# Smaller score tiles in all steps but the first, and a later load of one weight tile, in a fused attention and low-rank mixer kernel

## The chip, the cores and the metric

The kernel runs on one core of one Trainium2 chip. Its time is the device time in microseconds of one execution. The engines are named as in the profile: PE is TensorE (matmuls), PEld its weight loads, DVE is VectorE, ACT is ScalarE, POOL is GpSimd, and SP is the engine whose queue issues nearly all DMAs here.

## The reference

Two blocks follow each other. The first is causal linear attention with decay, by blocks, for 4 batches, 8 heads, 768 positions and a head width of 64. The second takes its result x (4 x 768 x 512), adds a low-rank mix over positions, and applies a two-layer network with a residual.

```python
for b in range(nb):
    intra = np.einsum('bhic,bhjc->bhij', qb, kb) * Dmask[None]
    intra = np.einsum('bhij,bhjd->bhid', intra, vb)
    inter = np.einsum('bhid,bhde->bhie', qb * lam_pow[None], kv_state)
    out[:, :, sl] = intra + inter
    kv_state = lam_block[None, :, None, None] * kv_state + np.einsum('bhsd,bhse->bhde', kb_dec, vb)
...
h = xt @ U @ V
u = x + h.transpose(0, 2, 1)
ch = np.maximum(u @ w_ch1, 0.0) @ w_ch2
return (u + ch).astype(np.float32)
```

q, k, v and lam are 32-bit floats. U, V, w_ch1 and w_ch2 come as 64-bit floats (two 32-bit words each).

## The kernel before

**Attention, steps 0 to 23.** The kernel works on 128 positions at a time (not the reference's 64): step s is batch s // 6 and position tile s % 6, with all 8 heads. For each step PE does, in small fp32 matmuls:

- `prep`: transposes of the raw q and k tiles (L355), which ACT copies to SBUF (L358);
- `scores`: q times k for every head (L400), into the PSUM tile pss;
- `masked`: DVE multiplies pss by the decay mask into sm (L409), in two halves, x = 0 and 1;
- `inter`: the part from the running state (L441), which needs the state kv and the scaled q (qs, by POOL, L383);
- `intra`: sm times v (L453), added in the same PSUM tile px, which ACT copies to x_nat (L458);
- `state`: the new state (L418 on PE, L426 on DVE).

From step 6 on the mixing of the batch before runs beside it: `low` (L469, once per batch), `mix` (L514 on PE, L517 on DVE: x_nat is changed in place), and `turn`, which transposes (L531), splits into high and low parts (L536, L547 on DVE, L550 on ACT, L551 on POOL), and writes u_d back to DRAM (L534 on SP).

The order on every engine is written out by hand in the list `pieces`. In step s come: prep of s+1, mix, intra of s, state of s, the late ACT work, scores of s+1, inter and masked of s+1, turn. So the scores and the mask of a step are computed one step ahead. SP issues DMAs in this program order too; q and v have three buffers and k has four, so a load is issued when an older tile is free, about three steps before its use.

**The scores' tiles.** A head has 64 columns of q and k, so two heads share the 128 partitions (x selects the half). Up to step 11 one matmul takes 64 rows and 128 columns of weights; from step 12 (`s >= 2 * NT`) it is split in two of 64 x 64, each writing half of the output's partitions. The number of passes per fp32 matmul is two, so the profile counts twice the instructions of the source.

**The weight tiles.** The first network's weights w_ch1 are converted from 64-bit words to three 32-bit parts by `w1_steps`. Its pieces are, for tile 0: four loads of 128 KB (L140), then "one" (L160 and L149 on DVE, and two ACT operations for the exponents, L167 and L168), "two" (L178), "three" (L186), "four" (L191), "five" (L209, then an ACT copy L212), "six" (L217) and "seven" (L224). For tile 1 the second half of "one", `mantissa` (L149), is a piece of its own. The table `side` says in which step each piece runs. `aside(s)` executes those of step s: for s < 12 after `masked`, from step 12 on before `inter` and `masked` (ahead of L409 on DVE). ACT operations of a piece are put on the list `late` and executed in the next step, after its `turned` piece. "One" waits for all four loads.

After step 23 come the first product (L732, L742 on PE, for all of w_ch1, with the conversion of further tiles beside it) and the second product (L865, L867, L869).

Of the kernel before, what the change touches and what calls it, by code (L numbers as in the profile page):

```python
# [14 lines left out]
P = 128  # L15
# [3 lines left out]
def kernel(  # L19
# [32 lines left out]
    NT = S // P  # L52
# [7 lines left out]
    NS = B * NT  # L60
# [136 lines left out]
    def split_steps(tile_of, src, in_parts=False, scale=None, apart=False):  # L197

        st = {}

        def dst():
            if "w" not in st:
                st["w"] = wconv.tile([P, C], FP32, tag="wf", name="wf")
            return st["w"]

        def five():
            st["t"] = t = wconv.tile([P, C], FP32, tag="wt", name="wt")
            st["o"] = o = tile_of()
            nc.vector.tensor_scalar(  # L209
                t.bitcast(U32), st["w"].bitcast(U32), HI, None, ALU.bitwise_and  # L210
            )
            on_scalar(lambda: nc.scalar.copy(o[:, 0, :], t))  # L212

        def six():
            w, low = st["w"], st["o"][:, 1, :]
            st["low"] = low.bitcast(FP32) if scale is None else w
            nc.vector.tensor_tensor(  # L217
                out=low if scale is None else w, in0=w, in1=st["t"], op=ALU.subtract
            )
            if scale is not None:  # L220
                on_scalar(lambda: nc.scalar.mul(low, w, scale))

        def seven():
            nc.vector.scalar_tensor_tensor(  # L224
                st["o"][:, 2, :], st["t"], -E, st["low"], ALU.mult, ALU.add
            )

        return weight_steps(dst, src, C, in_parts=in_parts, apart=apart) + [five, six, seven]
# [3 lines left out]
    def w1_steps(ft, in_parts=False, apart=False):  # L232
        def tile_of():
            w1v[ft] = w1_pool.tile([P, 3, C], F32R, tag="w1", name="w1")
            return w1v[ft]

        cols = moe_w_ch1[:, ft * P : (ft + 1) * P].rearrange("(c p) f -> p c f", p=P)
        return split_steps(tile_of, cols, in_parts, apart=apart)
# [13 lines left out]
    def two_banks(name, tag):  # L252
        return psf.tile([P, 2, N], FP32, tag=tag, name=name)
# [83 lines left out]
    half = [slice(0, D), slice(D, P)]  # L337
# [56 lines left out]
    def scores(s):  # L394
        qt, kt = st[s]["qt"], st[s]["kt"]
        st[s]["pss"] = pss = two_banks("pss", "pss").rearrange("p x (a i) -> p x a i", a=HP)
        for a in range(HP):
            for x in range(2):
                for rows in half if s >= 2 * NT else [slice(0, P)]:
                    nc.tensor.matmul(  # L400
                        out=pss[rows, x, a, :], lhsT=kt[half[x], a, rows],
                        rhs=qt[half[x], a, :], start=True, stop=True,
                    )
# [182 lines left out]
    def load_next(name, engine=nc.sync):  # L586
# [3 lines left out]

    run = {
        "prep": prep, "fade": fade, "scores": scores, "masked": masked, "inter": inter,
        "intra": intra, "state": state,
        "low": low, "low_rows": low_rows, "next_of_low": next_of_low, "mix": mix, "turn": turn,
        "scale": scale, "turned": lambda s: turned.pop(s)(),
    }
    def v_steps():

        st = {}

        def dst():
            if "v" not in st:
                st["v"] = wconv.tile([P, C], FP32, tag="wf", name="vf")[0 : 2 * R, 0:SH]
            return st["v"]

        def parts(gs):
            for half in range(2):
                rows, cols = slice(half * R, (half + 1) * R), slice(half * SH, (half + 1) * SH)
                for g in gs:
                    yield v_hl[g * R : (g + 1) * R, cols], rows  # L610

        def five():
            st["t"] = t = wconv.tile([P, C], FP32, tag="wt", name="vt")[0 : 2 * R, 0:SH]
            nc.vector.tensor_scalar(
                t.bitcast(U32), st["v"].bitcast(U32), HI, None, ALU.bitwise_and
            )
            on_scalar(lambda: high(0))

        def high(g, copy=nc.scalar.copy):
            for out, rows in parts((g,)):  # L620
                copy(out, st["t"][rows])

        def low(g, engine):
            for out, rows in parts((g,)):
                engine.tensor_tensor(
                    out=out, in0=st["v"][rows], in1=st["t"][rows], op=ALU.subtract
                )

        halves = [moe_V[:, half * SH : (half + 1) * SH] for half in range(2)]
        return weight_steps(dst, halves, SH, 2 * R, in_parts=True) + [  # L630
            five, lambda: low(1, nc.vector), lambda: high(2, nc.vector.tensor_copy),
            lambda: low(3, nc.gpsimd),
        ]
# [6 lines left out]
    for steps, at in (  # L640
        (u_side, (-1, 1, 1, 2, 2)),
        (v_steps(), (0, 0, 3, 3, 4, 4, 4, 5, 4, 5)),
        (w1_steps(0, True), (3, 4, 5, 6, 8, 9, 10, 11, 13, 14, 15)),
        (w1_steps(1, True, True), (8, 9, 10, 11, 16, 17, 19, 20, 21, 22, 23, NS)),
    ):
        assert len(steps) == len(at)
        for step, n in zip(steps, at):
            side.setdefault(n, []).append(step)
# [320 lines left out]
```

## Time and profile before

| | |
|---|---|
| Median of 3 runs | 673.42 us (672.98 to 673.69) |
| The profiled execution: time, span | 673.08 us, 671.3 us |
| Busy: PE, PEld, DVE | 665.1, 544.9, 497.1 us |
| Busy: ACT, POOL | 277.3, 112.1 us |
| Granted PE clock | 1.00 |
| PE, scores L400: 64 x 128 tiles, 64 x 64 tiles | 192 of 297 ns, 384 of 275 ns |
| DVE, mask L409 | 48, 30.9 us |
| SP, words L140: 128 KB | 8 issues, 4.0 us to landing (median) |
| Attention's last L453 begins | 119.2 us |

The engines run side by side, so the times are not added. An engine's idle time is put down in brackets to what released it, in the form "[0.24 <-DVE ut L536]". In the timeline the first column is the start in microseconds from the span's beginning and the second the time it took; "x16" is the number of instructions merged into one line. "SPq" is SP's queue of DMA issues, and its time is that of the issue, not of the transfer.

### The profile page before, as it was taken

How to read it: one execution, taken by the hardware profiler on the slowest of the kernel's cores; microseconds unless marked ns; L12 is line 12 of the kernel's file. 1: busy time of each engine (PE TensorE's matmuls, PEld its weight loads, DVE VectorE, ACT ScalarE, POOL GpSimd, SP SyncE). 2: the span in 40 equal slices, each digit the busy share in tenths (PEclk: the TensorE clock that was granted, in tenths of full speed). 3: DMA queues.
4: the chain of work that ended last, by engine and by line, in shares of the span. 5: the costliest groups of instructions: out<-in, count | busy, mean ns of one | idle time of the engine just before them, and what ended most of it. 6: DMA issues, size and time to landing. Idle time of an engine off the chain costs nothing.

```text
span 671.3 us, 13171 instructions
## 1 busy us (share of the span) xinstructions
PE 665.1 (99%) x5124; PEld 544.9 (81%) x5124; DVE 497.1 (74%) x873; ACT 277.3 (41%) x517; POOL 112.1 (17%) x92
## 2 busy tenths in 40 slices
PE   9999999999999999999999999999999999999997
PEld 7888989788888888888888888888888888888886
DVE  4689989877999777777797255786586775865864
ACT  4675767454555444444454121232222322322320
POOL 4465667340000000000000000030030300300300
PEclk9999999999999999999999999999999999999999
DMA  8999993254776555555577899854363363543431
GB/s 198 218 247 239 225 231 113 90 208 157 244 273 234 205 203 205 204 204 205 203 282 254 318 319 388 287 178 151 94 217 97 112 203 94 168 146 95 159 92 63
DMA packets 131775, 131.27 MB, mean 196 GB/s; under 512 B 81346, under 2 KB 89794, under 8 KB 131714
## 3 DMA queue, kind: packets, MB, share of 16 engines
q1 hardware_dynamic: 130512, 130.05, 61.2%
q8 instruction: 40, 0.66, 0.4%
q10 hardware_dynamic: 1202, 0.39, 0.2%
q14 instruction: 21, 0.17, 0.1%
HBM read 80.09 MB, written 50.33 MB: 194 GB/s over the span
## 4 chain that ended last, share of the span: by engine, by line
PE 97%; DVE 1%; DMA 1%; ACT 0%; issue 0%; ACTq 0%; DVEq 0%
PE pz L732 27%; PE pz L867 13%; PE pd L742 13%; PE pz L865 13%; PE pd L869 13%; PE px L453 4%; PE pss L400 4%; PE put L531 2%; PE pq L355 2%; PE px L441 2%; PE pk L355 1%; PE pkv L418 1%; PE pp L469 1%; PE pu L514 1%; DMA kraw<-in_k_dram 1%
## 5 line engine op out<-in xcount | busy, mean ns | idle before, releaser
L732 PE MATMUL pz<-u_hl,w 128*128 128x512 f32 x768 | 190.4, 397 | 0.0
L732 PEld LDWEIGHTS pz<-u_hl,w 128*128 128x128 f32 x768 | 144.0, 188 | 35.4 <-issue 0.4
L867 PE MATMUL pz<-w_hl,m 128*128 128x512 f32 x384 | 151.1, 396 | 0.0
L865 PE MATMUL pz<-w_hl,m 128*128 128x512 f32 x384 | 150.9, 396 | 0.0
L869 PE MATMUL pd<-w_d,m 128*128 128x512 f32 x384 | 149.5, 396 | 0.0
L848 ACT ACTIVATE m<-mt 128x512 fp32r<-128x512 f32 x96 | 60.5, 632 | 197.0 <-PE pd L869 148.9
L849 DVE SCALAR_TENSOR_TENSOR m<-rm,m 128x512 fp32r<-128x512 f32 x96 | 71.4, 746 | 53.7 <-ACT m L848 53.6
L894 POOL TENSOR_TENSOR o<-o,u 128x512 f32<-128x512 f32 x20 | 29.8, 1522 | 447.4 <-DVE o L890 447.4
L747 DVE SCALAR_TENSOR_TENSOR r<-pd,r 128x512 f32<-128x512 f32 x96 | 61.8, 686 | 53.2 <-ACT r L738 38.8
L742 PE MATMUL pd<-u_d,w 128*128 128x512 f32 x384 | 98.6, 397 | 0.0
L738 ACT ACTIVATE r<-pz 128x512 f32<-128x512 f32 x96 | 52.1, 596 | 92.7 <-PE pz L732 92.6
L867 PEld LDWEIGHTS pz<-w_hl,m 128*128 128x128 f32 x384 | 72.3, 188 | 17.7
L865 PEld LDWEIGHTS pz<-w_hl,m 128*128 128x128 f32 x384 | 72.3, 188 | 17.6
L869 PEld LDWEIGHTS pd<-w_d,m 128*128 128x128 f32 x384 | 72.3, 188 | 17.6
L742 PEld LDWEIGHTS pd<-u_d,w 128*128 128x128 f32 x384 | 72.1, 188 | 17.3
L850 DVE SCALAR_TENSOR_TENSOR m<-m 128x512 fp32r<-128x512 f32 x96 | 69.0, 721 | 0.9
L847 DVE TENSOR_SCALAR mt<-rm 128x512 uint32<-128x512 uint32 x96 | 46.1, 481 | 27.3 <-DMA rm<-r_d 26.9
L409 DVE TENSOR_TENSOR sm<-pss,mask 128x512 f32<-128x512 f32 x48 | 30.9, 685 | 7.9 <-PE pss L400 7.7
L212 ACT CAST w<-wt 128x512 fp32r<-128x512 f32 x32 | 19.9, 620 | 30.6 <-DVE wt L209 23.4
L383 POOL TENSOR_TENSOR qs<-qt,powq 128x512 f32<-128x512 f32 x20 | 26.0, 1298 | 22.0 <-ACT qt L358 19.0
L453 PEld LDWEIGHTS px<-vraw,sm 128*64 128x64 f32 x768 | 24.5, 138 | 5.2 <-issue 2.0
L400 PE MATMUL pss<-qt,kt 64*64 64x128 f32 (+1 forms) x576 | 28.1, 283 | 0.0
(88 smaller groups left out, 682.3 us busy)
## 6 DMA issues: line engine op xcount, KB each, us to landing
r_d<-r SPq DMA_DIRECT2D x96, 256.0 KB, 2.5
rm<-r_d SPq DMA_DIRECT2D x96, 256.0 KB, 2.7
words<-in_moe_w_ch_dram SPq DMA_DIRECT2D x30, 512.0 KB, 4.4
w_d<-w SPq DMA_DIRECT2D x16, 768.0 KB, 3.3
w_hl<-w_d SPq DMA_DIRECT2D x16, 512.0 KB, 6.6
vraw<-in_v_dram SPq DMA_DIRECT2D x24, 256.0 KB, 4.8
u_d<-x_nat SPq DMA_DIRECT2D x24, 256.0 KB, 3.6
u<-u_d SPq DMA_DIRECT2D x24, 256.0 KB, 3.8
```

Of the source, the lines that this page charges most:

```text
L400: nc.tensor.matmul(out=pss[rows, x, a, :], lhsT=kt[half[x], a, rows], rhs=qt[half[x], a, :], start=True, stop=True,)
L453: nc.tensor.matmul(out=px[half[t], x, a, :], lhsT=sm[:, x, a, half[t]], rhs=vr[:, 2 * a + x, :], start=(first and a == 0), stop=(a == HP - 1),
L732: nc.tensor.matmul(out=acc[g][0], lhsT=w[:, n, ct, :], rhs=uhl[g][:, n, ct, :], start=(ct == 0 and n == 0), stop=(ct == CT - 1 and n == 1),)
L738: nc.scalar.mul(rs[g], acc[g][0], 4096.0 + 1.0)
L742: nc.tensor.matmul(out=acc[g][1], lhsT=w[:, 2, ct, :], rhs=ud[g][:, ct, :], start=(ct == 0), stop=(ct == CT - 1),)
L747: nc.vector.scalar_tensor_tensor(rs[g], acc[g][1], 4096.0, rs[g], ALU.mult, ALU.add)
L848: nc.scalar.activation(out=m[:, 0], in_=t, func=AF.Relu)
L849: nc.vector.scalar_tensor_tensor(m[:, 1], r, 0.0, hi, ALU.max, ALU.subtract)
L850: nc.vector.scalar_tensor_tensor(m[:, 2], hi, E, low, ALU.mult, ALU.subtract)
L865: nc.tensor.matmul(out=pz, lhsT=m[:, 0, cols], rhs=hl[:, 0], start=first, stop=False)
L867: nc.tensor.matmul(out=pz, lhsT=m[:, 1, cols], rhs=hl[:, 1], start=False, stop=end)
L869: nc.tensor.matmul(out=pd, lhsT=m[:, 2, cols], rhs=dd, start=first, stop=end)
```

## The change

It has three parts. The scores are computed on 64 x 64 tiles in every step but step 0 (before: from step 12 on). The four loads of the words of weight tile 1 run in steps 11 to 14 (before: 8 to 11). "Seven" of tile 0 goes from step 15 to 16, and "one" of tile 1 from step 16 to 15. All else, the order of the other pieces included, stays.

```diff
-                for rows in half if s >= 2 * NT else [slice(0, P)]:
+                for rows in half if s > 0 else [slice(0, P)]:
                     nc.tensor.matmul(
                         out=pss[rows, x, a, :], lhsT=kt[half[x], a, rows],
                         rhs=qt[half[x], a, :], start=True, stop=True,
...
-        (w1_steps(0, True), (3, 4, 5, 6, 8, 9, 10, 11, 13, 14, 15)),
-        (w1_steps(1, True, True), (8, 9, 10, 11, 16, 17, 19, 20, 21, 22, 23, NS)),
+        (w1_steps(0, True), (3, 4, 5, 6, 8, 9, 10, 11, 13, 14, 16)),
+        (w1_steps(1, True, True), (11, 12, 13, 14, 15, 17, 19, 20, 21, 22, 23, NS)),
```

## The prediction

> **What bounds the kernel now.** I read the busy line and the chain of the page first, then the groups by form, the timeline of two neighbouring steps, and the waits.
>
> ```profile
> PE 665.1 (99%) x5124; PEld 544.9 (81%) x5124; DVE 497.1 (74%) x873; ACT 277.3 (41%) x517; POOL 112.1 (17%) x92
> ...
> PE 97%; DVE 1%; DMA 1%; ACT 0%; issue 0%; ACTq 0%; DVEq 0%
> ```
>
> TensorE (PE) is never free: it is busy 99% of the span and is 97% of the chain. After 119 us its waits add up to under 2 us. So what the attention part (0 to 119 us, steps 0 to 23) saves on PE should arrive at the end, unless another engine makes PE wait. Below, "step s" is the time from the first L453 matmul of step s to that of s+1; it holds the scores of s+1.
>
> The groups by form show what an L400 instruction costs in both tilings, and the timeline shows step 9 (old form) and step 13 (new form):
>
> ```profile
> L400 PE MATMUL pss<-qt,kt 64*128 64x128 f32 x192 | 14.9, 297 | 0.0
> ...
> L400 PE MATMUL pss<-qt,kt 64*64 64x128 f32 x384 | 13.2, 275 | 0.0
> ...
> 53.08 1.16 PE L400 MATMUL pss<-qt,kt 64*128 64x128 f32 x16
> ...
> 54.80 0.66 PE L531 MATMUL put<-ident,x_nat 128*128 128x128 f32 x4
> ...
> 73.34 1.10 PE L400 MATMUL pss<-qt,kt 64*64 64x128 f32 x32
> ...
> 74.84 0.66 PE L531 MATMUL put<-ident,x_nat 128*128 128x128 f32 x4
> ```
>
> Reader: a line's first number is its start. From the first score to the first matmul after L441 it is 54.80 - 53.08 = 1.72 us in the old form and 74.84 - 73.34 = 1.50 in the new, twice the instructions notwithstanding: **0.21 us a step**. Whole steps agree: 4.95 us (51.53 to 56.49) against 4.73 (71.80 to 76.53), with the same other work on PE.
>
> VectorE (DVE) is the engine that can eat it. In steps 5 and 6 it runs without a gap from 30.87 to 42.37:
>
> ```profile
> 38.34 0.42 DVE L489 TENSOR_SCALAR p_h<-p_f 32x512 uint32<-32x512 uint32 x1
> ...
> 39.17 1.19 DVE L495 TENSOR_TENSOR vp<-p_f,p_h 32x512 fp32r<-32x512 f32 x1
> ...
> 40.40 1.29 DVE L409 TENSOR_TENSOR sm<-pss,mask 128x512 f32<-128x512 f32 x2
> ...
> 41.57 1.06 PEld L453 LDWEIGHTS px<-vraw,sm 128*64 128x64 f32 x32 [0.25 <-issue]
> ```
>
> L409 ends at 41.69; the L453 that reads it began at 41.57 and took 1.06 us instead of its usual 1.01. There PE already runs at DVE's pace.
>
> The third place is where the words of the second weight tile are read:
>
> ```profile
> 65.28 0.79 SPq L140 DMA_DIRECT2D words<-in_moe_w_ch_dram  x1
> ...
> 78.19 2.16 SPq L279 DMA_DIRECT2D vraw<-in_v_dram  x1
> ...
> 80.46 0.79 SPq L534 DMA_DIRECT2D u_d<-x_nat  x1
> ...
> 83.00 0.43 DVE L426 TENSOR_TENSOR kv<-pkv,faded 128x256 f32<-128x256 f32 x1
> ...
> 83.34 0.68 DVE L224 SCALAR_TENSOR_TENSOR w<-wt,w 128x512 fp32r<-128x512 f32 x1
> ...
> 87.74 0.42 DVE L426 TENSOR_TENSOR kv<-pkv,faded 128x256 f32<-128x256 f32 x1 [0.54 <-PE pkv L418]
> ...
> 88.08 0.66 DVE L160 TENSOR_SCALAR sc<-words 128x512 uint32<-128x512 uint32 x1
> ...
> 94.94 1.25 PEld L469 LDWEIGHTS pp<-x_nat,u_w 128*32 128x32 f32 x48 [0.64 <-ACT qt L358]
> ```
>
> The last words were issued at 65.28, far ahead of L160 at 88.08. The bracket on L469 is a wait of PE on ScalarE (ACT) in step 17.
>
> **What the Trainium skill says.** "TensorE: Matmul & The Clock Gate", section The mechanism: tiles at different positions of the array compute at once, and a weight load overlaps matmuls in flight only when its row group differs. The trace agrees that it pays: 32 matmuls of 275 ns need less time than 16 of 297. "Runtime: NRT & Kernel Launch", Instruction fetch mechanics: instructions come in blocks of 16 KiB, 256 each, fetched by DMA while the current ones run, "mostly hidden". The trace has 40 instruction packets of 0.66 MB together, 16 KiB each, and one PE stall that nothing else explains, 0.53 us at 22.0, 2 us after a late packet at 20.35. "SBUF — State Buffer", Who interferes with whom: a DVE operation with two SBUF inputs is held up by a GpSimd (POOL) operation. The trace agrees: L186 takes 0.68 us alone and 1.36 beside L372 at 60.45.
>
> **The change part by part.**
>
> *Scores 1 to 11.* They add 11 x 8 = 88 matmuls, 176 records in the page's count (two per matmul), and as many weight loads. Gross gain 11 x 0.21 = 2.3 us. What of it stays:
> - Scores 1 to 5 (steps 0 to 4): 5 x 0.21 = 1.05. Here the inputs are close behind: raw v of step 4 was issued at 21.87 and took 5.3 us, landing at 27.17, and is needed at 28.11 - 4 x 0.21 = 27.27. q of step 3 lands at 16.84 and is needed at 17.66 - 0.42 = 17.24. Both just hold. Instruction blocks come faster: a step of 105 matmuls and 105 loads becomes 242 instructions in 4.08 us, so 256 last about 4.3 us instead of 5.2. The existing stall may move, vanish or double: from -0.5 (then v of step 4 binds instead) to +0.8. I charge 0.1 and count 0.95.
> - Scores 6 and 7 (steps 5, 6): nothing. DVE's gapless chain from 30.87 to 41.69 keeps its length, so the L453 of step 7 waits what PE saved, up to 0.42.
> - Scores 8 to 11 (steps 7 to 10): 4 x 0.21 = 0.84. DVE has room: 3.4 to 4.3 us busy of 4.74, and each L409 still waits 0.6 for its scores. Step 11's wait of 0.41 on x_nat keeps its distance to scores 11.
>
> *Operation "seven" (L224) from step 15 to 16, "one" (L160) from 16 to 15.* On DVE 0.68 against 0.43 to 0.66, a swap. The two exponents on ACT (L167, L168, 0.72 each) go with "one" and run a step later in its late list: now in step 17, 92.95 to 94.42, delaying the copy of q (L358) that pp L469 waits for; afterwards in step 16, where ACT idles 1.92 us before L358. The copy then starts when its transposes end, near 94.0 instead of 94.33: **gain 0.3**.
>
> *Words from steps 8 to 11 to 11 to 14.* Four issues on SP of 128 KB. Steps 8 to 10 lose one each, which nobody waited for. In steps 12 to 14, SP issues q, k, v and u_d for 0.39 + 0.65 + 2.15 + 0.88 = 4.1 us of 4.73; another 0.8 to 1.1 fills it, so u_d, and next q, slip by under 1 us. q and k are three steps ahead of their use, and the u_d write two steps ahead of the reuse of its buffer, so these are hidden. But the **fourth words** are issued in step 14 behind v, at about 80.4 to 80.9 on the old clock, and landed after 3.0 to 4.8 us in the eight old cases: 83.4 to 85.7. L160 now stands where L224 began, 83.4. It waits 0 to 2.3 us; I take 1.2 (landing 84.6). Behind it on DVE stand sm (L409), ut, u_hl, x_nat and kv. L160 ends at 84.6 + 0.66, sm's second half at 86.57; L453 wants it 0.13 after 86.00: PE stalls 0.45. kv then ends near 88.9, where L441 starts at 88.82 after that stall: 0.15 more. **Loss 0.6**. Up to a wait of some 0.55 the slack of DVE (0.54 before kv at 87.74, 0.7 before L453) covers it; a wait of 2.3 costs 1.7.
>
> Sum: -0.95 - 0.84 - 0.30 + 0.60 = **-1.5 us**. The profiled execution took 673.08, 1.8 us of it outside the span of 671.3; it becomes 671.6. It lies 0.34 below the median of the three runs, 673.42, so the median becomes **671.9**.
>
> **The rivals.** "Within 0.2%" means 672.07 to 674.77; 0.2%, 1.35 us, is about what a measurement of this kernel can tell from no change.
> 1. *The words are hidden*: they land by 84.0. Then the 0.6 is not paid: -2.1, and with luck at scores 6 and 7, -2.4. About 671.2. For it: the lighter queue in steps 8 to 10, and a landing of 3.4 us at 65.28. Against: v's issue of 2.16 shows the rings full there. Chance 0.27.
> 2. *The early part is fed too slowly*: v of step 4 or instruction blocks absorb half of the first 0.95, and the words wait 2 us (1.4). Sum -0.5 - 0.84 - 0.30 + 1.4 = -0.2, with part of it -0.8: 672.9. Tiles that bring nothing under full DMA rings, so that the change does not do what it says, end here too. Chance 0.20.
> 3. *Slower: instruction fetch.* Counting 256 records back from the stall puts the request of the late block near 17.7, so it was some 4.8 us until use (an estimate). Blocks now last 4.3 us in steps 1 to 4 and about 4.8 in 5 to 11. If the mean delay under DMA traffic is above 5.2, each of some ten blocks stalls 0.4 to 0.5: +4.5 against -1.5: 676.4. The sign turns from about four stalls on; it is slower by 0.2% from seven. Against: steps 12 to 18, already 252 instructions per 4.73 us at a DMA share of about 1.0, show no such stall. Chance 0.08.
>
> **How the numbers follow.** Likeliest, with 0.45: 671.9, its own range 671.3 to 672.5, two thirds of it below 672.07. Faster: 0.27 + 0.30 = 0.57; same: 0.15 + 0.20 = 0.35; slower 0.08. The range 670.9 to 673.3 takes in rivals 1 and 2 and leaves out the slower case and the ends.
>
> **What would show it.** Right: steps 7 to 10 last 4.74 us; the L453 of step 7 shows a wait of 0.3 to 0.4 on sm L409; L160 stands behind kv in step 15 with idle time put down to the words' DMA; L469 of step 17 waits 0.3 instead of 0.64. Wrong: PE waits put down to issue at several places before 60 us (rival 3), L453 waiting for vraw (rival 2), no idle before L160 (rival 1), or steps of 64x64 scores before step 12 that stay at 4.9 us.

## The result, and the profile after

The changed kernel takes 676.71 us (median of 22 runs, 674.39 to 680.7) against 673.74 us (22 runs, 672.59 to 678.36) for the kernel before on the same chip: ratio 1.004, interval 1.0026 to 1.0054. The forecast was 671.9, with a range of 670.9 to 673.3; the outcome is the one that the prediction gave 0.08. The profiled execution of the changed kernel took 678.94 us with a span of 677.2.

First the page of the kernel after, its busy line and its chain, against those shown of before:

```profile
PE 665.6 (98%) x5300; PEld 544.9 (80%) x5300; DVE 497.8 (74%) x873; ACT 277.8 (41%) x517; POOL 112.8 (17%) x92
...
PE 94%; DMA 2%; ACT 1%; issue 1%; DVE 1%; SPq 0%; DVEq 0%; ACTq 0%
```

The 176 records more are there (5124 to 5300), yet PE is not busier: 665.1 to 665.6. The span grew by 5.9 us, nearly all of it waiting. From the first L732 to the end both take the same, 550.9 and 551.0 us, so everything lies in attention: from its first to its last L453 it went from 109.19 to 115.62 us.

The groups by form and the waits of the kernel after (name, waited-for: total us, times, longest) say that the tiles are as fast as forecast, and where PE stands instead:

```profile
L400 PE MATMUL pss<-qt,kt 64*64 64x128 f32 x736 | 25.9, 276 | 0.8 <-issue 0.8
```

```profile
PEld px L441 <- issue: 5.8, 6, 1.7
```

276 ns each, as before (275). But L441 waited six times for nothing that the profile shows. The timeline of PEld in the kernel after gives the places (start, time, what, and in brackets the idle time before it):

```profile
21.18 0.52 PEld L400 LDWEIGHTS pss<-qt,kt 64*64 64x64 f32 x18 [1.03 <-issue]
...
40.36 0.54 PEld L441 LDWEIGHTS px<-kv,qs 64*64 64x64 f32 x26 [1.15 <-issue]
...
45.51 0.43 PEld L441 LDWEIGHTS px<-kv,qs 64*64 64x64 f32 x20 [0.56 <-issue]
...
56.63 0.59 PEld L441 LDWEIGHTS px<-kv,qs 64*64 64x64 f32 x32 [1.73 <-issue]
...
76.93 0.47 PEld L441 LDWEIGHTS px<-kv,qs 64*64 64x64 f32 x20
78.84 0.31 PEld L441 LDWEIGHTS px<-kv,qs 64*64 64x64 f32 x12 [1.44 <-issue]
...
84.22 0.31 PEld L441 LDWEIGHTS px<-kv,qs 64*64 64x64 f32 x11 [0.47 <-issue]
...
91.49 0.90 PEld L453 LDWEIGHTS px<-vraw,sm 128*64 128x64 f32 x28 [0.27 <-DVE sm L409]
...
100.09 1.25 PEld L469 LDWEIGHTS pp<-x_nat,u_w 128*32 128x32 f32 x48 [0.37 <-ACT qt L358]
...
104.98 0.20 PEld L441 LDWEIGHTS px<-kv,qs 64*64 64x64 f32 x5 [0.48 <-issue]
```

The reader is to see that most stalls fall in the **middle** of a group of equal instructions (20 of 32 L441, a pause of 1.44 us, the other 12). Data are not what is missing there: the other 12 read the same two tiles as the first 20. The exception is 56.63, ahead of a whole group: that one is kv, late by way of ACT and u_d, told below.

Counting PE's records (matmuls and weight loads) from the start, the pauses within a group stand at 688, 1444, 1700, 1952, 3469, 3720 and 4732: 688 plus a multiple of 252.8 to within three records. The trace also holds PE's semaphore instructions (about three per step), which the views leave out. Counted with them, the seven pauses lie 3, 1, 1, 6, 1 and 4 times 256 apart, exactly: **every 256 instructions, the block of the instruction fetch**. So do the pauses put down to "issue" in the middle of a group in all other kernels of this document. One more view ties a pause to its packet, the DMA queues of the kernel after from 75.7 to 77.5 us (packets, MB, share of 16 engines):

```profile
q8 instruction: 1, 0.02, 5.2%
```

5.2% of 16 engines for 1.8 us is 1.5 us for this packet on its one engine; narrower windows put its start at 75.80, so it ended at 77.3, and PE went on at 78.84. The same in every such pause of the kernel after: PE goes on 1.2 to 1.6 us after the end of a packet. In the kernel before one packet was late in this way (timeline of PEld, before):

```profile
22.54 0.19 PEld L441 LDWEIGHTS px<-kv,qs 64*64 64x64 f32 x3 [0.67 <-issue]
```

After, the pauses of this kind sum to 5.4 us (the seventh, not shown above, is 0.27 in an L469 at 35.30).

### The profile page after: what moved, and what is told of

It is laid out like the page before. It is cut to its first block, busy times and chain, and to the rows that moved or that the text cites. A ratio compares the mean times of both kernels' runs of the same rounds, so it can differ in the third digit from the quotient of the medians.

```text
span 677.2 us, 13523 instructions
## 1 busy us (share of the span) xinstructions
PE 665.6 (98%) x5300; PEld 544.9 (80%) x5300; DVE 497.8 (74%) x873; ACT 277.8 (41%) x517; POOL 112.8 (17%) x92
## 4 chain that ended last, share of the span: by engine, by line
PE 94%; DMA 2%; ACT 1%; issue 1%; DVE 1%; SPq 0%; DVEq 0%; ACTq 0%
PE pz L732 27%; PE pz L867 13%; PE pd L742 13%; PE pz L865 13%; PE pd L869 13%; PE px L453 3%; PE pss L400 3%; PE put L531 2%; PE pq L355 1%; PE px L441 1%; PE pkv L418 1%; PE pk L355 1%; PE pp L469 1%; DMA qraw<-in_q_dram 1%; DMA u_d<-x_nat 1%
## 5 line engine op out<-in xcount | busy, mean ns | idle before, releaser
L732 PE MATMUL pz<-u_hl,w 128*128 128x512 f32 x768 | 190.5, 397 | 0.0
L732 PEld LDWEIGHTS pz<-u_hl,w 128*128 128x128 f32 x768 | 144.0, 188 | 35.5 <-issue 0.4
L453 PEld LDWEIGHTS px<-vraw,sm 128*64 128x64 f32 x768 | 24.6, 138 | 5.7 <-DVE sm L409 2.3
```

The lines of the kernel that those rows point to most:

```text
L732: nc.tensor.matmul(out=acc[g][0], lhsT=w[:, n, ct, :], rhs=uhl[g][:, n, ct, :], start=(ct == 0 and n == 0), stop=(ct == CT - 1 and n == 1),)
```

## The experiments

"First to last" is the time from the first to the last L453 of the profiled execution. "Delay" is the time from PE's first instruction of a new block (by the count with the semaphore instructions) to the start of the next instruction packet. The "rings" are the queues in which the pieces of the transfers wait for the DMA engines. Ratios are to the kernel before in the same session, as recorded, with their 95% interval; they are not exactly the quotients of the medians. Steps, pauses and delays are those of one profiled execution of each kernel.

**Each part alone.** `e1_scores_only` keeps the score tiles only (`half if s > 0`, the table `side` as before); `e2_moves_only` keeps the words and the exchange only (`s >= 2 * NT`).

> Only the first part of the change: scores 1 to 11 on 64 x 64 tiles; words and the two operations as before. Fetch theory (PE waits at the ends of 256-instruction blocks because full DMA rings delay the next block, and the added instructions use blocks up faster): nearly the whole loss, +1.5 to +4 us against before, with waits put down to issue about 253 records apart. Words theory (the later loads of the words and what they displace in the DMA queue make the loss): -1.5 to -2.3 us.

> Only the second and third part: words in steps 11 to 14, L224 and L160 exchanged; scores as before. Fetch theory: within 0.6 us of before (0.3 gained at L469 of step 17, up to 0.6 lost at L160). Words theory: +2 to +4 us.

e1: 675.27 against 672.32 us, ratio 1.0039 (1.0026 to 1.0052). e2: 673.17, ratio 1.0011 (0.9998 to 1.0025). So the scores' tiles, the part meant to save most, make the whole loss. Steps without a pause do save: steps 1 to 3 of e1 last 4.07 to 4.08 instead of 4.29. But e1 pauses at records 1952, 3217, 4226 and 4733, for 0.99, 0.26, 0.72 and 1.07 us. e2 has no pause of the kind, and shows the wait for the words on the way that was forecast, but nearly twice as long. Its timelines of DVE and of PEld:

```profile
83.97 0.43 DVE L160 TENSOR_SCALAR sc<-words 128x512 uint32<-128x512 uint32 x1 [2.12 <-DMA words<-in_moe_w_ch_dram]
```

```profile
85.05 0.20 PEld L453 LDWEIGHTS px<-vraw,sm 128*64 128x64 f32 x4 [0.87 <-DVE sm L409]
...
85.64 0.90 PEld L453 LDWEIGHTS px<-vraw,sm 128*64 128x64 f32 x28 [0.40 <-DVE sm L409]
```

L160 waits 2.12 us, both halves of sm come late, and steps 15 and 16 take 5.37 and 5.25 us instead of 4.73 and 4.74: 1.15 lost.

**Larger pieces.** `e3_after_2k_rows` (the changed kernel) and `e4_before_2k_rows` (the kernel before) read q, k and v as whole rows of 2 KB instead of 8 pieces of 256 B (the tiles then hold other values; no instruction of PE changes):

```diff
-                in_=source[b, h : h + n, c * P : (c + 1) * P, :].rearrange("h p d -> p h d"),
+                in_=source[b].rearrange("h s d -> (h s d)")[
+                    (c * H + h) * P * D : (c * H + h + n) * P * D
+                ].rearrange("(p h d) -> p h d", h=n, d=D),
```

> The changed kernel, but the loads of q, k and v read 2 KB contiguous rows instead of 256-byte pieces: same bytes, an eighth of the descriptors, other data in the tiles, so the attention computes on other values; no instruction of PE, DVE, ACT or POOL is changed. Fetch theory: the DMA share falls well below 1, the waits at block ends vanish, and the kernel is 1.5 to 2.3 us faster than the kernel before with the same loads. Words theory: the same, as the words land early too; then the wait of L160 goes. A theory by which the 64 x 64 form itself is slow in the early steps: still slower than the kernel before with 2 KB rows by 2 us or more.

> The kernel before with the same 2 KB rows for q, k and v (other data in the tiles, as in the run beside it). Fetch theory: its one late block (0.53 us) goes and little else changes, -0.3 to -1.5 us. If the DMA rings bound the early steps in other ways, more.

e3: 672.92, ratio 1.0003 (0.9992 to 1.0014); e4: 671.78, ratio 0.9986 (0.9978 to 0.9994). Lighter traffic takes most of the loss away, but the changed kernel stays the slower one, and still pauses four times (0.85, 0.44, 0.75, 0.42). Traffic has a share; packets do not simply stand behind many small pieces, for the mean delay in steps 12 to 22 is 1.79 us with 2 KB rows and 1.78 without.

**How many instructions, and where a block ends.** From step 12 on a step has 250 records and mostly three semaphore instructions, almost one block, so the end of a block stays near one place of the step. In the kernel before this is in L453, 0.8 us into the step; 352 instructions more (one block and 96) bring it into L441, at 2.8 us. `e5_eight_steps` adds exactly one block (64x64 tiles also in steps 2 to 5 and 8 to 11). `e6_place_only` adds 96 instructions that do nothing, ahead of attention (25 small matmuls in place of one larger idle one), and changes no tile. `e7_eight_steps_swap` is e5 with L224 in step 16 and L160 in step 15, words in 8 to 11. `e8_all_steps_place` has small tiles in all steps but the first and 160 idle instructions ahead of them (42 small matmuls for two larger ones), which bring the end of the block back into L453.

```diff
+                for rows in half if s >= 2 * NT or s in (2, 3, 4, 5, 8, 9, 10, 11) else [slice(0, P)]:   # e5, e7
...
+    for i in range(25):                                            # e6; e8: 42
+        nc.tensor.matmul(out=fill[0:32, 0:2], lhsT=blank[:, 0:32], rhs=blank[:, 0:2], start=True, stop=True)
```

> The kernel before with the new tiles in eight of the eleven steps only, scores 2 to 5 and 8 to 11: 8 x 32 = 256 more instructions on PE, exactly one block, so that from step 12 on the block ends fall at the same place in a step as in the kernel before. Place theory (a block waits when its end falls among the L441, since the request for the next block then queues behind the loads of v): steps 12 to 22 last 4.73 to 4.74 us as before, and the kernel is 0.5 to 1.7 us faster than before. Rate theory (more instructions per microsecond are the cause): stalls in steps 1 to 11 as in the run with all eleven, and a loss of 1 to 2.5 us.

> The kernel before with scores, words and conversion untouched, and 96 more PE instructions ahead of the first transposes: 25 dummy matmuls of 32 x 2 for one dummy matmul of 128 x 128 taken away (about 0.9 us against some 1 us). In the change the 352 added instructions move the block ends of the later steps by 352 - 256 = 96, and here they move by the same. Place theory: waits at block ends in steps 8 to 19 though no rate is changed, 1 to 3 us slower than before. Rate theory: within 0.6 us of before, no new waits.

> As the eight steps, and L224 in step 16 and L160 in step 15 as in the change, but the words stay in steps 8 to 11. L160 should find its words there; the wait of L469 in step 17 falls from 0.64 to 0.37. Both theories: 0.3 us faster than the eight steps alone. If the exchange itself costs DVE time, slower than the eight steps.

> All eleven new score steps (words and conversion as before), and 160 more PE instructions ahead of the first transposes (42 dummy matmuls of 32 x 2 for two of 128 x 128): 352 + 160 = 512, two whole blocks, so the later block ends lie as in the kernel before. Place theory: steps 12 to 22 without waits at block ends, 1 to 2 us faster than the run with the scores alone. Rate theory: as slow as the scores alone (+2.6 us).

e5: 672.59 against 672.64, ratio 1.0003 (0.999 to 1.0016). e6: 676.31, ratio 1.0055 (1.0041 to 1.007). e7: 672.35, ratio 1.0002 (0.9989 to 1.0015). e8: 674.56, ratio 1.0031 (1.002 to 1.0043). Of the two forecasts for e5 neither came true: it is as fast as the kernel before. Its steps 12 to 22 are as they were (but for step 17, 5.99), yet in the early steps a pause of 0.83 at 30.12 and the longer steps 11 and 17 take back most of what its tiles save. The fillers cost more than I had thought: the first L453 of e6 starts at 12.45 and of e8 at 13.83, where the others have 8.5 to 11.0. So these two medians are no measure of the place; the steps are. e6 does the very same work as the kernel before, and gets two pauses that it does not have (timelines of PEld, e6):

```profile
71.85 0.32 PEld L441 LDWEIGHTS px<-kv,qs 64*64 64x64 f32 x14 [0.47 <-issue]
```

```profile
102.00 0.20 PEld L441 LDWEIGHTS px<-kv,qs 64*64 64x64 f32 x6 [0.52 <-issue]
```

Steps 12 and 18 take 5.39 and 5.44 instead of 4.74. Its first to last is 109.58, only 0.4 above the kernel before, as it lacks that one's early pause: so the two pauses, 1.35 us by the steps, are the place's doing, and most of the 3.7 us between the medians is not (its first L453 starts 2.45 us later). e8 has all the small tiles of the changed kernel and no pause after 25.61; its first to last is 107.17, the shortest of all kernels with every load, 4.2 below e1. Its lead in the prologue helps its first steps, so not all of the 4.2 is the place's doing; but its steps 13 to 22 are clean, and those of e1 are not.

`e9_nine_steps` and `e10_ten_steps` move the place without fillers; `e11_swap_only` is the kernel before with the exchange alone.

```diff
+                for rows in half if s >= 2 * NT or s in (1, 2, 3, 4, 5, 8, 9, 10, 11) else [slice(0, P)]:   # e9; e10: 6 too
...
-        (w1_steps(0, True), (3, 4, 5, 6, 8, 9, 10, 11, 13, 14, 15)),
-        (w1_steps(1, True, True), (8, 9, 10, 11, 16, 17, 19, 20, 21, 22, 23, NS)),
+        (w1_steps(0, True), (3, 4, 5, 6, 8, 9, 10, 11, 13, 14, 16)),      # e7, e9, e10, e11
+        (w1_steps(1, True, True), (8, 9, 10, 11, 15, 17, 19, 20, 21, 22, 23, NS)),
```

> The kernel before, with 64x64 score tiles also in steps 1 to 5 and 8 to 11 (288 instructions of TensorE more, 256 + 32), L224 in step 16 and L160 in step 15, the words' loads where they were (steps 8 to 11). From step 12 on a block of 256 instructions then ends some 32 instructions earlier in each step than before, near position 14, at the start of L453. If the place of the block's end decides (theory): steps 12 to 22 stay at 4.73 to 4.74, as that place is still ahead of v's load; the steps 0 to 10 gain 0.21 each less what one or two early stalls take, 671.3 to 672.2 against 672.6 before. If the rate alone decides (rival): stalls as in the changed kernel in steps 7 to 13, 2 to 3 us slower.

> As the nine steps, with step 6 too (320 instructions more, 256 + 64): a block then ends some 64 instructions earlier in each step, near position 234, behind L441, among the transposes for the next step. Theory: the next block is asked for about when v's 1024 pieces are in the rings, so stalls of 0.4 to 0.7 come in two or more of the steps 7 to 20, 1 to 3 us slower than the nine steps although the code differs by 32 instructions. Rival (rate): within 0.3 us of the nine steps.

> The kernel before with the exchange alone: L224 in step 16, L160 in step 15, words' loads in steps 8 to 11, scores as before (no instruction of TensorE more). Step 17 loses 0.26 to 0.3, L160 waits for no DMA, everything else as before: 0.2 to 0.4 us faster than before. Its distance to the run that moved the words too (0.5 us over before) is then the price of the later words, 0.7 to 1.0. Rival: L160 ahead of L409 in step 15 delays sm, so that step 15 takes 0.2 to 0.4 more and nothing is gained.

e9: 673.16 against 673.45, ratio 0.9999 (0.9983 to 1.0016). e10: 675.01, ratio 1.002 (1.0008 to 1.0031). e11: 673.12, ratio 0.9992 (0.9979 to 1.0004). Thirty-two instructions in step 6 part e9 from e10 by 1.9 us. e9 has no pause of the fetch in attention, e10 four (0.48, 0.82, 0.82 and 0.49), two of them in steps 7 and 13, as the theory of the place wanted; beyond step 13 it has none. The gain that I expected of e9 did not come: steps 3, 9 and 10 lose it again (4.82, 5.43, 5.69) to waits for other engines. The one of step 9 is put down to "issue", but it stands ahead of a whole group, not at the end of a block, and ACT had waited for u_d just before (timelines of ACT and PEld, e9):

```profile
51.23 0.58 ACT L458 COPY x_nat<-px 128x512 f32<-128x512 f32 x1 [1.85 <-DMA u_d<-x_nat]
```

```profile
51.88 0.59 PEld L441 LDWEIGHTS px<-kv,qs 64*64 64x64 f32 x32 [0.66 <-issue]
```

It is the same chain as at 56.63 in the kernel after. In the profiled execution e10 also waited 1.61 us for a q tile in step 0, so its first to last (111.59) overstates the pauses. e11 gains in step 17 what was forecast (5.38 instead of 5.65), and its L160 waits for no DMA. By medians e2 lies 0.2% above e11 (1.0011, 0.9992; the intervals overlap a little); 0.2% would be about 1.2 us for the later words, as against 1.15 in e2's steps.

**Does the place matter because of v's load?** My next theory was that a block ending in L441 asks for the next one just when the 1024 pieces of v's load, issued behind the state's matmuls, fill the rings. Moving only that issue to the end of the step tests it: `e12_after_v_late` in the changed kernel, `e13_all_v_late` the same with the words' loads in steps 8 to 11, `e14_swap_v_late` in e11.

```diff
-        load_next("v")
+        if s < 5:
+            load_next("v")
...
+        step += [("load_v", s)] * (s >= 5)      # last in the step, behind turn
```

> The changed kernel with v's load issued at the end of a step, behind u_d, instead of behind the state's matmuls, from step 5 on. If the instruction packet queues behind v's pieces (theory): the block that ends in L441, some 3.3 us into the step, is now followed by a request ahead of v's pieces, the packets of steps 12 to 22 start within 4 us of the step instead of 4.5 to 6.1, and the stalls of 0.47 to 1.44 in steps 9 to 18 go: 2 to 4 us faster than the changed kernel, 673 to 674.5. Rival (it is the rate, or L441 itself): the same stalls, 676 to 677.

> As the last one, with the words' loads back in steps 8 to 11 (all steps on 64x64 tiles, the exchange, v's load late). Theory: no L160 wait, no stalls from step 8 on; 0.7 to 1.0 below the last one, 672 to 673.5. Rival: stalls as before, 675 to 676.

> The kernel before with the exchange and v's load issued at the end of a step from step 5 on; TensorE's instructions as in the kernel before, so a block ends in L453 at the start of a step, now just behind the issue of v's load. Theory: the packets of steps 12 to 22 start later in the step, at 3 to 5 us instead of 1.0 to 2.4, and stalls of 0.4 to 1 appear in two or more steps: 0.5 to 3 us slower than the exchange alone. Rival: no change, within 0.3 us of it.

e12: 676.1 against 674.47, ratio 1.004 (1.0025 to 1.0055); e13: 676.43, ratio 1.0039 (1.0019 to 1.006); e14: 673.26, ratio 0.9984 (0.9971 to 0.9997). **The theory falls**, in both directions. e12 keeps the loss and has the longest pause of all (timeline of PEld, e12; L442 is L441 here):

```profile
106.06 0.20 PEld L442 LDWEIGHTS px<-kv,qs 64*64 64x64 f32 x4 [2.09 <-issue]
```

and e14, whose requests should have come to stand behind v, has no pause of the fetch and the best ratio of the kernels that leave the loads as they are in kind and number, though not one that its interval tells from e11's. The mean delay does not move as the theory wants: 2.04 in e12 (changed kernel: 1.78), 1.10 in e14 (e11: 0.85).

**Queueing at all?** `e15_after_no_v` is the changed kernel without v's loads from step 9 on, `e16_after_no_qkv` without those of q, k and v, `e17_before_no_qkv` the kernel before without them (older tiles are used again, so they compute on other values).

```diff
     def load(name, s, engine):
+        if s >= 9:                       # e15: and name == "v"
+            raw[s, name] = kept[name, s % (4 if name == "k" else 3)]
+            return
```

> The changed kernel without v's loads from step 9 on (the tiles of steps 6 to 8 are used again, so x is another one); TensorE's instructions as in the changed kernel. If the packets wait among data in the rings (theory, without v's special part): the mean delay from block end to packet in steps 12 to 22 falls from 1.9 to about 1.2 us, no stall put down to issue from step 12 on: 2 to 3 us faster than the changed kernel. Rival (the delay comes from the engine's side): still 1.6 to 2.2 us.

> As the last one, with no load of q, k or v from step 9 on: only u_d and the words use the rings. Theory: mean delay under 0.8 us, packets of 0.9 us, no stall from step 9 on, steps 12 to 22 at 4.73. Rival: mean delay still 1.6 to 2.2 us; a stall would then still come now and then.

> The kernel before without loads of q, k and v from step 9 on: the other place of the block end, with empty rings. Theory: mean delay 0.3 to 0.8 us, as in the changed kernel without these loads (the place no longer matters), where the kernel before has 1.0. Rival: 1.0, unchanged, or under half of what the changed kernel without the loads shows.

e15: 672.45 against 673.46, ratio 0.9982 (0.9968 to 0.9997); e16: 671.18, ratio 0.997 (0.9958 to 0.9981); e17: 670.91, ratio 0.9962 (0.9947 to 0.9977). The DMA queues of the kernel after from 74 to 98 us (steps 13 to 16) and of e16 from 60 to 100 us (steps 11 to 19), in packets, MB and share of 16 engines, show how empty the rings became:

```profile
q1 hardware_dynamic: 15549, 5.34, 87.5%
```

```profile
q1 hardware_dynamic: 1584, 2.49, 17.9%
```

With it the mean delay falls from 1.78 (kernel after) to 1.05 (e15) and 0.30 (e16), and the pauses from step 12 on from 2.4 us to 0.26 and none. So the delay depends on the data in the rings: e15 and e16 as expected, far below the rival's 1.6. By medians e16 and e17 differ by 0.3 us (671.18, 670.91): without the loads the loss is gone, but the forecast gain does not show either. These kernels have fewer semaphore instructions (e16 and e17 mostly one in a step), so their blocks hold more records, and the ends of blocks move on in the step. The delays in steps 12 to 22 together (10 or 11 blocks each):

| Kernel | Block ends, us into the step (median) | Mean delay (largest) | Pauses from step 12 on |
|---|---|---|---|
| before | 0.8 | 1.05 (2.40) | none |
| e8, all small tiles, place moved back | 0.8 | 0.82 (1.91) | none |
| e9, nine steps | 0.3 | 1.11 (1.69) | none |
| e14, exchange, v late | 0.8 | 1.10 (2.14) | none |
| e17, before without q, k, v | 1.1 | 0.36 (0.73) | none |
| after | 2.8 | 1.78 (3.38) | 1.44, 0.47, 0.48 |
| e1, scores only | 2.8 | 1.76 (3.19) | 0.26, 0.72, 1.07 |
| e3, after, 2 KB rows | 2.8 | 1.79 (2.39) | 0.75, 0.42 |
| e6, place only | 2.8 | 1.69 (2.13) | 0.47, 0.52 |
| e10, ten steps | 3.9 | 1.29 (3.08) | 0.49 |
| e12, after, v late | 2.8 | 2.04 (4.14) | 0.58, 2.09 |
| e13, as e12, words in 8 to 11 | 2.8 | 1.66 (3.02) | 0.53, 0.26 |
| e15, after without v | 2.9 | 1.05 (1.68) | 0.26 |
| e16, after without q, k, v | 3.4 | 0.30 (1.15) | none |

A block must be there one block after it was asked for. Delay, packet (0.9 to 2.4 us) and the 1.2 to 1.6 us behind it must fit into the block that runs meanwhile. In the pause at 78.84: 3.38 + 1.49 + 1.4 = 6.27 us, where the block that ran meanwhile lasted from 72.43 to 77.40, 4.97 us: 1.30 too late; the pause is 1.44. In e12 at 106.06: 4.14 + 1.59 + 1.4 - 4.92 = 2.21; it is 2.09. The rule sorts all 396 blocks of attention in the 19 traces of this case. Where a packet ended over 1.5 us before the running block ran out, PE never stood at the block's end for more than the 0.24 us that it spends ahead of L453 anyway (335 blocks); where it ended under 1.1 us before, PE always paused, by over 0.2 us (33 blocks); in between 7 of 28 paused. Where a batch's first tile brings in the dense L469 (48 pairs in 1.25 us), the block that begins there, in steps 11 and 17, lasts only 3.7 to 3.9 us until L441 of the next step: hence the pauses in steps 12 or 18 of e1, e3, e6, e12, e13, e15 and the kernel after, mostly with quite ordinary delays.

What stays open is why the delay behind L441's place is nearly twice that behind L453's. It is not when v's load is issued (e12, e14), nor the size of the pieces (e3). The traffic is only part of it. In steps 12 to 15, where e16's blocks still end in L441, its mean delay is 0.82 and that of e17, in L453 or just behind, 0.29 (four blocks each); with the loads, 2.17 in the kernel after and 1.05 before. So about half of the difference stays when the loads are gone. In e16 the delay then falls to -0.41 as the ends move on to 4.7 us into the step: the packet starts before PE has come to the block's end, so what asks for it runs ahead of PE. How far ahead it is at each place would be a candidate for the rest; no run here tests it. Which transfers share an engine with the instruction packets the trace's views do not tell.

## Why the prediction was wrong, point by point

**What failed.** The step "Instruction blocks come faster ... I charge 0.1 and count 0.95", and the sentence that held rival 3 down: "steps 12 to 18, already 252 instructions per 4.73 us at a DMA share of about 1.0, show no such stall". The observation was right and the inference wrong. These steps were clean not because their rate is harmless, but because their blocks ended where packets start early (mean 1.05 us), so that 1.05 + 1.13 (packet) + 1.4 = 3.6 us had to fit into 4.75; e6 has the same rate and pauses. The change adds one block and 96 instructions *ahead* of them; untouched steps 13, 14 and 18 lose 2.4 us in three pauses. I had costed the added instructions only in the steps that hold them. In place of the 0.1, the pauses of the profiled execution cost 4.7 us more than before. Rival 3's 676.4 came close to the median of 676.71, but by luck: its mechanism, ten pauses once the mean exceeds 5.2 us, was not what happened. In steps 12 to 22 the mean is about 1.8 + 1.3 + 1.4 = 4.5, and seven times in attention the sum exceeded its own block, of 3.7 to 5.2 us. On this point "mostly hidden" in the Trainium skill ("Runtime: NRT & Kernel Launch", Instruction fetch mechanics) is what I leaned on; here the measurement decides, up to 1.44 us of PE at the end of one block.

**Scores 1 to 5, 8 to 11.** The size was right: a step without a pause saves 0.21 to 0.22 (e1: 4.07 for 4.29; e5 and e8: 4.73 and 4.74 for 4.95). In the kernel after only step 3 keeps all of it (4.07); steps 2 and 7, for instance, pause 1.03 and 0.56. "Both just hold" was right for v of step 4, for which nothing waited, and wrong for q of step 3: L355 waits 0.41 us for it at 17.16.

**Scores 6 and 7.** Next to nothing, as forecast: steps 5 and 6 of e8, which has the new tiles there and no pause, last 4.59 and 4.45, before 4.65 and 4.52. DVE's chain holds: its row in e8 has no gap from 33.69 to beyond 44.

**Step 11.** "Step 11's wait of 0.41 on x_nat keeps its distance" did not hold in general: with PE earlier, L531 waits 0.83 to 0.84 in e5, e7 and e10, and step 11 takes 6.05 instead of 5.62, two steps' savings gone. In the kernel after and in e9 the wait is not there, 5.39, but step 12 then takes 4.94 for 4.74: DVE's row from 69.69 to 74.56 has no gap.

**The exchange.** Forecast 0.3, measured 0.26: L469 of step 17 waits 0.37 instead of 0.64 (100.09 above), in e2, e7 and e11 too.

**The words.** Forecast: a wait of 1.2 and a loss of 0.6, with the way from L160 over sm to L453. Measured: 2.12 and 1.15 in e2; in the kernel after a wait of 0.84 (timeline of DVE, after) and 0.4 lost in step 16.

```profile
89.29 0.95 DVE L160 TENSOR_SCALAR sc<-words 128x512 uint32<-128x512 uint32 x1 [0.84 <-DMA words<-in_moe_w_ch_dram]
```

The route was right. That the kernel after waits less fits the pauses ahead of it, which give the words time: DVE came to L160 6.6 us later than in e2, the words landed 5.3 us later.

**"so these are hidden" (u_d and q, in steps 12 to 14).** There nothing waited in the kernel after; u_d was missed earlier, in some executions. In the kernel after, in step 9 SP, held by k issues of 2.2 to 2.5 us, issued the u_d of the first turn at 50.83 (before: 45.33), and ACT, which needs the x_nat buffer that this write reads, waited for it (timeline of ACT, after):

```profile
55.98 0.59 ACT L458 COPY x_nat<-px 128x512 f32<-128x512 f32 x1 [2.91 <-DMA u_d<-x_nat]
```

Behind it stood `faded`, kv and the L441 at 56.63: 1.73 us. e9, e12 and e14 have the same wait of ACT in step 9, of 1.85, 1.45 and 1.34 us; in e9 PE then stands 0.66. How often the changed kernel meets it one trace cannot tell; at this size it may be one reason why the profiled execution (678.94) lies above the median.

**The sum.** Forecast -1.5, measured +3.0 by medians. In the profiled execution: pauses of the fetch +4.7 (5.4 less 0.67), kv in step 9 +1.7, the words +0.4, the exchange -0.3: 6.5 of the 6.4 us between first and last L453. The tiles' gain, -1.9, is offset by smaller waits, in steps 0, 1, 10 and 12 above all. That is a second failure of the sum: even in kernels without the loss (e5, e7, e9) the gain does not reach the median.

## What to carry to other kernels

When a change adds instructions to a saturated engine, count them in blocks of the instruction fetch, and ask where the blocks end in the code *behind* the change, too: code that is not touched can begin to stall. A clean stretch is no proof that its rate of instructions is safe under busy DMA queues; compare the time of a block with delay, packet and the 1.4 us measured behind it here, and look for pauses put down to "issue" in the middle of a group. Here a whole block more (e5, e7) cost nothing, 32 instructions further (e10 against e9) 1.9 us, and the best that the runs showed with all loads as they are is the exchange with v's load moved (e14, 0.9984), which the noise does not tell from the exchange alone (e11, 0.9992).

## What had not been expected of the hardware

PE goes on 1.2 to 1.6 us after the end of an instruction packet, in all 40 pauses of over 0.2 us at the ends of blocks. A packet of 16 KB takes 0.9 us on its engine at best and up to 2.36 us under load (e5). The mean delay ahead of it is 0.30 and 0.36 us with nearly empty rings (e16, e17) and 0.8 to 2.0 with all loads, up to 4.14 (e12). Pauses stand a multiple of 256 TensorE instructions apart in every kernel, about 252.8 records of the views where a step has three semaphore instructions, so a pause can be told from a data wait by counting.
